# Three chunks instead of four under thirteen first-layer blocks, and two loads moved behind weights: a fused attention + MLP kernel on one core

## The chip, the core and the metric

One core of a Trainium2 chip. The metric is device time in microseconds (us) of one execution; the trace's span, from the first to the last instruction, is 2.0 to 2.2 us shorter in all traces but one. In the traces PE is TensorE, PEld its weight loads, DVE VectorE, ACT ScalarE, POOL GpSimd and SP SyncE.

## The reference

Lightning attention with a decay per head, then a two-layer MLP with an exact Gelu:

```python
# q, k, v: (4 batches, 8 heads, 768, 64); lam: (8,); block = 64
for b in range(nb):
    intra = einsum('bhic,bhjc->bhij', qb, kb) * Dmask      # lam ** (i - j), causal
    out_b = einsum('bhij,bhjd->bhid', intra, vb) + einsum('bhid,bhde->bhie', qb * lam_pow, kv_state)
    kv_state = lam**block * kv_state + einsum('bhsd,bhse->bhde', kb * rev_pow, vb)
x = out.transpose(0, 2, 1, 3).reshape(3072, 512)
h = x @ w_in                                               # 512 -> 2048
out = (0.5 * h * (1 + erf(h / sqrt(2)))) @ w_out           # 2048 -> 512
```

## The kernel before

The kernel works in chunks of 128 positions of one batch: chunk n is batch n % 4, positions from 128 * (n // 4). Four chunks (one of each batch) make a group of 512 tokens, and there are six groups. TensorE runs the MLP of one group as a list of blocks, and between them "visits" do the attention of the next group. Group 0 has nothing to hide its attention under, so its first blocks start on three chunks (384 columns), and the columns of the fourth, chunk 3, are made up later in "leftover" blocks.

```python
    for item in "q0 k1 q1 k2 q2 v1 v2".split():
        load(int(item[1]), item[0])                     # all from POOL, cast to bf16
...
    for piece in [(0, 2), (2, 5), "k", (5, 8), "q", (8, 10), "v", (10, 13), (13, 16)]:
        if piece in ("k", "q", "v"):
            load(3, piece)                              # k3, q3, v3
        else:
            load_w_in(*piece)                           # so many 128-column blocks of w_in
    for s in range(NS):
        load_w_out(s)
...
        split = {0: 10, 1: 8}.get(g, 0)
        blocks = [mm1(kf) for kf in range(NK2)]         # the first `split` on 384 columns
        for i, kf in enumerate(range(0, split, 4)):     # then their last 128 columns, four at a time
            blocks.insert(split + i, mm1(kf, T - C, min(4, split - kf)))
...
    def first_requests():
        for n in (2 * M, 2 * M + 1):                    # M = 4
            request(n)              # SP: kT by DMA transpose; POOL: q_hat; SP: qT by DMA transpose
        for n in range(M, 2 * M):
            decay_k(live[n], nc.gpsimd)                 # k_dec of chunks 4 to 7, on POOL
        prefetch(2 * M + 3)                             # loads of chunks 10 and 11
        for n in (2 * M, 2 * M + 1):
            decay_k(live[n], nc.gpsimd)
    visits = {
        (0, 5): [lambda: kv(0)],                        # before block 5 of group 0: state of chunk 0
        (0, 8): [lambda: transposes(live[3])],
        (0, 9): [lambda: scores(live[3]), lambda: decay_k(live[3], nc.vector)],
        (0, 10): [lambda: kv(1), lambda: outputs(live[3]), lambda: kv(2)],
        (0, 15): [lambda: kv(3)],
...
        (1, 6): [lambda: kv(4, 5)],
        (1, 8): [lambda: kv(6, 7)],
    }
```

`kv(n)` is four matmuls of k_dec and v, then on VectorE a multiplication, with an addition before it from chunk 4 on. k_dec is k times a decay; q_hat is q times a decay, and its DMA transpose is qT. Below "state" is `kv`, and "w_in(5,8)" the piece with blocks 5 to 7.

Of the kernel before, what the change touches and what calls it, by code (L numbers as in the profile page):

```python
# [15 lines left out]
def kernel(  # L16
# [10 lines left out]
    nc = tc.nc  # L27
# [66 lines left out]
        nc.gpsimd.dma_start(w_out_t[:, s * f:(s + 1) * f, :], w_out_r[:, s * f:(s + 1) * f, :])  # L94


    for piece in [(0, 2), (2, 5), "k", (5, 8), "q", (8, 10), "v", (10, 13), (13, 16)]:
        if piece in ("k", "q", "v"):
            load(3, piece)
        else:  # L100
            load_w_in(*piece)
# [53 lines left out]
    live = {}  # L155
# [10 lines left out]
    def decay_k(c, eng):  # L166

        if c.so < NB - 1:
            c.k_dec = work_pool.tile([128, H, D], BF16, tag="kd", name="k_dec", bufs=8)
            eng.tensor_mul(c.k_dec, c.k, lam_m[:, :, None].to_broadcast((128, H, D)))  # L170

    def transposes(c, between=lambda: None):

        t_ps = [bank([128, HP, C], BF16, "m" if c.n < 3 else "sc", "t_ps") for _ in range(2)]
        for dst, src in zip(t_ps, (c.k, c.q)):
            for hp in range(HP):
                nc.tensor.transpose(dst[:, hp, :], src[:, 2 * hp:2 * hp + 2, :], ident)  # L177
            if src is c.k:
                between()
        c.kT = work_pool.tile([128, HP, C], BF16, tag="kT", name="kT")  # L180
        c.qT = work_pool.tile([128, HP, C], BF16, tag="qT", name="qT")
        nc.scalar.copy(c.kT, t_ps[0])
        nc.vector.tensor_mul(c.qT, t_ps[1], lam_q)  # L183
# [9 lines left out]
    def scores(c):  # L193
        sc_ps = [bank([128, HP, C], F32, "sc", f"sc_ps{hi}") for hi in range(2)]
        for hp in range(HP):
            for hi in range(2):
                p = slice(hi * D, (hi + 1) * D)
                nc.tensor.matmul(sc_ps[hi][:, hp, :], c.kT[p, hp, :], c.qT[p, hp, :], start=True, stop=True)  # L198
        c.sc_m = work_pool.tile([128, HP, 2, C], BF16, tag="sc_m", name="sc_m")
        dmask_r = dmask.rearrange("p (hp hi) i -> p hp hi i", hi=2)  # L200
        for hi in range(2):
            nc.vector.tensor_mul(c.sc_m[:, :, hi, :], sc_ps[hi], dmask_r[:, :, hi, :])  # L202
# [18 lines left out]
    def inter(c):  # L221
        c.o_ps = bank([128, HP, C], F32, "sc", "o_ps")
        if c.so > 0:
            for hp in range(HP):
                nc.tensor.matmul(c.o_ps[:, hp, :], states[c.b][:, hp, :], c.qT[:, hp, :],  # L225
                                 start=(hp == 0), stop=False, skip_group_check=True)

    def intra(c):
        for hp in range(HP):
            for hi in range(2):  # L230
                nc.tensor.matmul(c.o_ps[hi * D:(hi + 1) * D, hp, :], c.v[:, 2 * hp + hi, :], c.sc_m[:, hp, hi, :],  # L231
                                 start=(c.so == 0 and hp == 0), stop=True, skip_group_check=True)
        x_o = xT[c.so][:, :, c.b * C:(c.b + 1) * C]
        if c.so < 2:
            nc.scalar.copy(x_o, c.o_ps)  # L235
        else:
            nc.vector.tensor_copy(x_o, c.o_ps)  # L237

    def outputs(c):
        inter(c)  # L240
        intra(c)
# [7 lines left out]
    def mlp_blocks(g):  # L249
        T = M * C  # L250

        split = {0: 10, 1: 8}.get(g, 0)
        x_t = xT[g]
        g_t = g_pool.tile([128, NK2, T], BF16, tag="g", name="g_t")

        def mm1(kf, lo=0, n_kf=1):

            hi = T - C if kf < split and lo == 0 else T
            def run():
                h_ps = bank([128, n_kf, hi - lo], F32, "m", "h_ps")  # L260
                for f in range(n_kf):
                    for ki in range(NK1):
                        w = w_in_t[:, ki, (kf + f) * 128:(kf + f + 1) * 128]
                        nc.tensor.matmul(h_ps[:, f, :], w, x_t[:, ki, lo:hi], start=(ki == 0 and f == 0),  # L264
                                         stop=(ki == NK1 - 1), skip_group_check=True)
                nc.scalar.activation(g_t[:, kf:kf + n_kf, lo:hi], h_ps, ACT.Gelu)  # L266
            return run, 4 * n_kf * (hi - lo)

        om = {}

        def mm2(io, part):
            def run():
                if part == 0:
                    om[io] = bank([128, d_model], F32, "m", "o2_ps")
                for kf in range(part * 4, part * 4 + 4):
                    nc.tensor.matmul(om[io], g_t[:, kf, io * C:(io + 1) * C], w_out_t[:, kf, :],  # L276
                                     start=(kf == 0), stop=(kf == NK2 - 1))
                if part == NK2 // 4 - 1:
                    o_sb = out_pool.tile([128, d_model], F32, tag="o_s", name="o_sb")
                    r = io * S + g * C  # L280
                    nc.scalar.copy(o_sb, om[io])  # L281
                    nc.sync.dma_start(out[r:r + C, :], o_sb)
            return run

        def mm2_cols(io, lo, hi):

            def run():
                o2 = bank([128, hi - lo], F32, "m", "o2_ps")
                for kf in range(NK2):
                    nc.tensor.matmul(o2, g_t[:, kf, io * C:(io + 1) * C], w_out_t[:, kf, lo:hi],  # L290
                                     start=(kf == 0), stop=(kf == NK2 - 1))
                o_sb = out_pool.tile([128, hi - lo], F32, tag=f"o_h{lo}", name="o_sb")
                r = io * S + g * C
                nc.scalar.copy(o_sb, o2)
                nc.sync.dma_start(out[r:r + C, lo:hi], o_sb)
            return run

        parts = NK2 // 4
        blocks = [mm1(kf) for kf in range(NK2)]
        for i, kf in enumerate(range(0, split, 4)):  # L300
            blocks.insert(split + i, mm1(kf, T - C, min(4, split - kf)))
        if g == 0:

            blocks += [(mm2(io, part), 4 * 512) for pair in range(0, M, 2) for part in range(parts)
                       for io in (pair, pair + 1)]
        else:
            last = g == NG - 1
            blocks += [(mm2(io, part), 4 * 512) for io in range(M - last) for part in range(parts)]
            if last:
                blocks += [(mm2_cols(M - 1, lo, hi), NK2 * (hi - lo)) for lo, hi in [(0, 384), (384, d_model)]]  # L310
        return blocks
# [8 lines left out]
    def keep_warm(n, new=True):  # L320

        if new:
            idle_ps[0] = bank([128, 512], F32, "m", "idle_ps")
        for _ in range(n):
            nc.tensor.matmul(idle_ps[0], idle[:, :128], idle, start=True, stop=True)  # L325
# [14 lines left out]
    transposes(live[1], lambda: keep_warm(1, new=False))  # L340
    keep_warm(2)
    outputs(live[0])
    transposes(live[2], lambda: keep_warm(1, new=False))
    nc.scalar.activation(warm, pos, ACT.Gelu)
    scores(live[1])
    keep_warm(1)
    scores(live[2])
    keep_warm(2)
    outputs(live[1])
    keep_warm(2)  # L350
    outputs(live[2])
    keep_warm(4)
    for n in range(M - 1):
# [22 lines left out]
    def kv(*ns):  # L376
        for n in ns:
            next_state(live[n])
            take_state(live[n])

    def first_requests():
        for n in (2 * M, 2 * M + 1):
            request(n)
        for n in range(M, 2 * M):
            decay_k(live[n], nc.gpsimd)
        prefetch(2 * M + 3)
        for n in (2 * M, 2 * M + 1):
            decay_k(live[n], nc.gpsimd)
# [1 line left out]

    visits = {
        (0, 5): [lambda: kv(0)],
        (0, 8): [lambda: transposes(live[3])],
        (0, 9): [lambda: scores(live[3]), lambda: decay_k(live[3], nc.vector)],
        (0, 10): [lambda: kv(1), lambda: outputs(live[3]), lambda: kv(2)],
        (0, 15): [lambda: kv(3)],
        (0, 27): [lambda: transposes(live[4])],
        (0, 29): [lambda: transposes(live[5])],
        (0, 30): [lambda: pair_a(4)],
        (0, 31): [lambda: transposes(live[6])],  # L400
        (0, 32): [lambda: first_requests()],
        (0, 33): [lambda: inter(live[4]), lambda: inter(live[5]), lambda: intra(live[4]), lambda: intra(live[5]),
                  lambda: scores(live[6])],
        (0, 34): [lambda: transposes(live[7]), lambda: outputs(live[6])],
        (1, 1): [lambda: scores(live[7])],
        (1, 4): [lambda: outputs(live[7])],
        (1, 6): [lambda: kv(4, 5)],
# [3 lines left out]
    def pair_a(n):  # L411
        for c in (live[n], live[n + 1]):
            scores(c)
# [68 lines left out]
```

## Time and profile before

| | value |
|---|---|
| time, first three runs | 213.76, 213.80, 214.01 us |
| time and span of the profiled run | 213.84, 211.8 us |
| TensorE busy | 203.2 us (96%) |
| start of the second-layer matmuls of group 0 ("second stage") | 33.69 us |
| from there to the end of the execution | 213.84 - 33.69 = 180.15 us |

The views are in the prediction. In the rows of a timeline L177 is transposes, L198 scores, L210 states, L225 and L231 outputs, L264 the first layer, L276 the second, L325 fillers (`keep_warm` in the kernel: matmuls without use), L170 k_dec and L190 q_hat.

### The profile page before, as it was taken

The numbers are of one execution on the slowest core, as the hardware profiler recorded it, in microseconds if no ns is written. First come the engines' busy times: TensorE is split into PE (matmuls) and PEld (weight loads), VectorE is DVE, ScalarE is ACT, GpSimd is POOL, SyncE is SP. The second block draws the span as 40 slices with busy tenths as digits, with TensorE's granted clock in tenths as the row PEclk, the third lists the DMA queues.
The fourth block names the chain that finished last, engine by engine and source line by source line (L and its number), as shares of the span: only waits on it lengthen the run. The fifth ranks groups of instructions, "written<-read, shape, count | busy, mean of one in ns | idle before, by whom it ended". The sixth has DMA issues, their size and how long they took to land.

```text
span 211.8 us, 3591 instructions
## 1 busy us (share of the span) xinstructions
PE 203.2 (96%) x1469; PEld 106.1 (50%) x1493; DVE 75.7 (36%) x122; ACT 87.7 (41%) x155; POOL 103.7 (49%) x119
## 2 busy tenths in 40 slices
PE   7898899999999999999999999999999999999994
PEld 2444564456674456444465444465444464444442
DVE  4782610173394036840414842244541240000000
ACT  5665553326665211466211465311466311566121
POOL 7994633891997957939795394941000000000000
PEclk9999999999999999999999999999999999999999
DMA  8999999999799799999989999999200012100112
GB/s 89 138 160 182 202 207 189 155 213 156 133 135 113 82 165 137 121 98 187 108 132 134 158 166 155 93 173 159 79 0 3 0 50 99 53 0 0 50 50 99
DMA packets 101327, 24.48 MB, mean 116 GB/s; under 512 B 92992, under 2 KB 98368, under 8 KB 101312
## 3 DMA queue, kind: packets, MB, share of 16 engines
q0 software_dynamic: 79120, 13.51, 86.1%
q1 hardware_dynamic: 22192, 10.76, 26.0%
q8 instruction: 11, 0.18, 0.4%
q14 instruction: 4, 0.03, 0.1%
HBM read 27.27 MB, written 6.29 MB: 158 GB/s over the span
## 4 chain that ended last, share of the span: by engine, by line
PE 87%; POOL 5%; DMA 4%; issue 1%; DVE 1%; ACT 0%; POOLq 0%
PE h_ps L264 37%; PE o_ps L276 37%; DMA w_in_t<-in_moe_w_in_dram 4%; PE sc_ps L198 3%; PE o_ps L231 3%; PE o_ps L225 2%; PE kv_ps L210 2%; POOL k_t L66 2%; PE o_ps L290 2%; POOL q_t L66 1%; PE t_ps L177 1%; POOL v_t L66 1%; POOL w_in_t L90 1%; DVE sc_m L202 1%; DVE qT L183 0%
## 5 line engine op out<-in xcount | busy, mean ns | idle before, releaser
L264 PE MATMUL h_ps<-x_t,w_in_t 128*128 128x512 bf16 (+2 forms) x446 | 86.2, 345 | 1.4 <-DMA w_in_t<-in_moe_w_in_dram 0.6
L276 PE MATMUL o_ps<-w_out_t,g_t 128*128 128x512 bf16 x355 | 81.2, 379 | 1.3 <-issue 1.0
L266 ACT ACTIVATE g_t<-h_ps 128x512 bf16<-128x512 f32 (+2 forms) x101 | 58.2, 577 | 33.8 <-PE h_ps L264 32.6
L264 PEld LDWEIGHTS <-w_in_t 128*128 128x128 bf16 x456 | 40.5, 98 | 41.2 <-DMA w_in_t<-in_moe_w_in_dram 1.1
L276 PEld LDWEIGHTS <-g_t 128*128 128x128 bf16 x368 | 35.0, 98 | 40.8
L202 DVE TENSOR_TENSOR sc_m<-sc_ps,dmask 128x512 bf16<-128x512 f32 x48 | 30.0, 685 | 41.5 <-PE sc_ps L198 41.5
L281 ACT COPY o_sb<-o_ps 128x512 f32<-128x512 f32 x23 | 13.5, 587 | 73.2 <-PE o_ps L276 69.7
L190 POOL TENSOR_TENSOR q_hat<-q_t,lam_p 128x512 bf16<-128x512 bf16 x16 | 16.9, 1056 | 27.3 <-issue 14.3
L66 POOL DMA_DIRECT2D k_t<-in_k_dram x24 | 22.1, 919 | 3.8 <-DMA w_out_t<-in_moe_w_out_dram 1.6
L66 POOL DMA_DIRECT2D q_t<-in_q_dram x24 | 21.6, 900 | 3.5 <-DMA w_out_t<-in_moe_w_out_dram 3.4
L66 POOL DMA_DIRECT2D v_t<-in_v_dram x23 | 20.8, 907 | 3.1 <-DMA w_out_t<-in_moe_w_out_dram 1.6
L170 POOL TENSOR_TENSOR k_dec<-k_t,lam_m 128x512 bf16<-128x512 bf16 x16 | 16.8, 1077 | 0.0
L237 DVE CAST x_t<-o_ps 128x512 bf16<-128x512 f32 x16 | 9.9, 684 | 18.1 <-PE o_ps L231 18.1
L217 DVE TENSOR_TENSOR tmp<-kv_ps,state 128x512 f32<-128x512 f32 x16 | 11.0, 686 | 12.2 <-PE kv_ps L210 12.2
L218 DVE TENSOR_TENSOR state<-tmp,lam_blk 128x512 bf16<-128x512 f32 x16 | 11.5, 719 | 0.6
L325 PE MATMUL idle_ps<-idle 128*128 128x512 bf16 x28 | 9.9, 476 | 1.2 <-DVE idle L106 1.2
L183 DVE TENSOR_TENSOR qT<-t_ps,lam_q 128x512 bf16<-128x512 bf16 x8 | 5.5, 691 | 15.3 <-PE t_ps L177 15.0
L198 PE MATMUL sc_ps<-qT,kT 64*128 64x128 bf16 x192 | 8.0, 217 | 0.7 <-DVE qT L183 0.4
L198 PEld LDWEIGHTS <-kT 64*128 64x128 bf16 x192 | 5.7, 94 | 5.9 <-issue 4.2
L231 PE MATMUL o_ps<-sc_m,v_t 128*64 128x128 bf16 x192 | 8.1, 222 | 0.4 <-DVE sc_m L202 0.2
L231 PEld LDWEIGHTS <-v_t 128*64 128x64 bf16 x192 | 5.9, 109 | 2.9 <-issue 1.7
L235 ACT CAST x_t<-o_ps 128x512 bf16<-128x512 f32 x8 | 4.6, 587 | 5.1 <-PE o_ps L231 5.0
(41 smaller groups left out, 72.1 us busy)
## 6 DMA issues: line engine op xcount, KB each, us to landing
out_dram<-o_sb SPq DMA_DIRECT2D x23, 256.0 KB, 2.2
k_t<-in_k_dram POOLq DMA_DIRECT2D x24, 128.0 KB, 4.7
q_t<-in_q_dram POOLq DMA_DIRECT2D x24, 128.0 KB, 5.7
v_t<-in_v_dram POOLq DMA_DIRECT2D x23, 128.0 KB, 6.5
w_out_t<-in_moe_w_out_dram POOLq DMA_DIRECT2D x4, 512.0 KB, 14.0
w_in_t<-in_moe_w_in_dram POOLq DMA_DIRECT2D x4, 384.0 KB, 9.6
w_in_t<-in_moe_w_in_dram POOLq DMA_DIRECT2D x2, 256.0 KB, 7.8
v_f<-in_v_dram SPq DMA_DIRECT2D x1, 256.0 KB, 3.6
```

The source lines that it names most:

```text
L66: nc.gpsimd.dma_start(raw[n, name], chunk_of(name, n))
L170: eng.tensor_mul(c.k_dec, c.k, lam_m[:, :, None].to_broadcast((128, H, D)))
L190: nc.gpsimd.tensor_mul(q_hat, c.q, lam_p[:, :, None].to_broadcast((128, H, D)))
L198: nc.tensor.matmul(sc_ps[hi][:, hp, :], c.kT[p, hp, :], c.qT[p, hp, :], start=True, stop=True)
L202: nc.vector.tensor_mul(c.sc_m[:, :, hi, :], sc_ps[hi], dmask_r[:, :, hi, :])
L217: nc.vector.tensor_add(tmp, kv_ps, states[c.b])
L218: nc.vector.tensor_mul(new, tmp, lam_blk)
L231: nc.tensor.matmul(c.o_ps[hi * D:(hi + 1) * D, hp, :], c.v[:, 2 * hp + hi, :], c.sc_m[:, hp, hi, :], start=(c.so == 0 and hp == 0), stop=T ...
L264: nc.tensor.matmul(h_ps[:, f, :], w, x_t[:, ki, lo:hi], start=(ki == 0 and f == 0), stop=(ki == NK1 - 1), skip_group_check=True)
L266: nc.scalar.activation(g_t[:, kf:kf + n_kf, lo:hi], h_ps, ACT.Gelu)
L276: nc.tensor.matmul(om[io], g_t[:, kf, io * C:(io + 1) * C], w_out_t[:, kf, :], start=(kf == 0), stop=(kf == NK2 - 1))
L281: nc.scalar.copy(o_sb, om[io])
```

## The change

The intent: take the waits out of group 0's first layer. w_in(5,8) goes ahead of k3, w_in(10,13) ahead of v3; thirteen blocks instead of ten run on three chunks, so that chunk 3's attention has more time; its visits are rearranged for that; and in the start chunk 1's scores are issued ahead of chunk 2's transposes.

```diff
-    for piece in [(0, 2), (2, 5), "k", (5, 8), "q", (8, 10), "v", (10, 13), (13, 16)]:
+    for piece in [(0, 2), (2, 5), (5, 8), "k", "q", (8, 10), (10, 13), "v", (13, 16)]:
@@
-        split = {0: 10, 1: 8}.get(g, 0)
+        split = {0: 13, 1: 8}.get(g, 0)
@@
     outputs(live[0])
+    scores(live[1])
     transposes(live[2], lambda: keep_warm(1, new=False))
     nc.scalar.activation(warm, pos, ACT.Gelu)
-    scores(live[1])
-    keep_warm(1)
-    scores(live[2])
     keep_warm(2)
     outputs(live[1])
-    keep_warm(2)
+    scores(live[2])
+    keep_warm(5)
     outputs(live[2])
@@
-        (0, 8): [lambda: transposes(live[3])],
-        (0, 9): [lambda: scores(live[3]), lambda: decay_k(live[3], nc.vector)],
-        (0, 10): [lambda: kv(1), lambda: outputs(live[3]), lambda: kv(2)],
-        (0, 15): [lambda: kv(3)],
-        (0, 27): [lambda: transposes(live[4])],
...
+        (0, 8): [lambda: transposes(live[3]), lambda: kv(1, 2), lambda: scores(live[3]),
+                 lambda: decay_k(live[3], nc.vector)],
+        (0, 12): [lambda: outputs(live[3])],
+        (0, 17): [lambda: kv(3)],
+        (0, 29): [lambda: transposes(live[4])],
...                     # chunks 4 to 7: each visit one or two blocks later; first_requests stays at 32
```

More of the change, by code (lines that the diff above doesn't have):

```diff
@@ L392 @@
         (0, 5): [lambda: kv(0)],
-        (0, 8): [lambda: transposes(live[3])],
-        (0, 9): [lambda: scores(live[3]), lambda: decay_k(live[3], nc.vector)],
-        (0, 10): [lambda: kv(1), lambda: outputs(live[3]), lambda: kv(2)],
-        (0, 15): [lambda: kv(3)],
-        (0, 27): [lambda: transposes(live[4])],
-        (0, 29): [lambda: transposes(live[5])],
-        (0, 30): [lambda: pair_a(4)],
-        (0, 31): [lambda: transposes(live[6])],
-        (0, 32): [lambda: first_requests()],
-        (0, 33): [lambda: inter(live[4]), lambda: inter(live[5]), lambda: intra(live[4]), lambda: intra(live[5]),
+        (0, 8): [lambda: transposes(live[3]), lambda: kv(1, 2), lambda: scores(live[3]),
[3 more added lines that the diff above has]
+        (0, 29): [lambda: transposes(live[4])],
+        (0, 31): [lambda: transposes(live[5])],
+        (0, 32): [lambda: pair_a(4), lambda: first_requests()],
+        (0, 33): [lambda: transposes(live[6])],
+        (0, 34): [lambda: inter(live[4]), lambda: inter(live[5]), lambda: intra(live[4]), lambda: intra(live[5]),
                   lambda: scores(live[6])],
-        (0, 34): [lambda: transposes(live[7]), lambda: outputs(live[6])],
+        (0, 35): [lambda: transposes(live[7]), lambda: outputs(live[6])],
         (1, 1): [lambda: scores(live[7])],
```

## The prediction

> **What bounds the kernel now.** I read the page first, then the list of waits, then TensorE's timeline from 9 to 64 us, then the landing time of each early transfer.
>
> ```profile
> PE 203.2 (96%) x1469; PEld 106.1 (50%) x1493; DVE 75.7 (36%) x122; ACT 87.7 (41%) x155; POOL 103.7 (49%) x119
> ...
> PE 87%; POOL 5%; DMA 4%; issue 1%; DVE 1%; ACT 0%; POOLq 0%
> ```
>
> TensorE is busy for 203.2 of 211.8 us, and the chain that ended last is 87% TensorE. The rest of that chain is the start: POOL issuing loads up to 11.14 us, then 8.70 us of waiting for w_in, so up to 19.84 us. So only two things can shorten the run: less work on TensorE, or fewer gaps in it. After 33 us the list of waits has one entry for TensorE, "issue" 1.0 us in six pieces. The other gaps are all before 33.5 us, where the change lies. The list of waits for 15 to 33.6 us, PE and its weight loads:
>
> ```profile
> PE h_ps L264 <- DMA w_in_t<-in_moe_w_in_dram: 0.6, 2, 0.4
> PE h_ps L264 <- ACT x_t L235: 0.3, 1, 0.3
> PE o_ps L231 <- DVE sc_m L202: 0.2, 1, 0.2
> ...
> PEld L264 <- DMA w_in_t<-in_moe_w_in_dram: 1.1, 2, 0.6
> ```
>
> These idle times are too short, because the end of each run of matmuls is modelled: the twelve from 17.16 are given 2.12 us, yet the next work starts 1.96 us after them. Distances between starts are safer. TensorE's timeline (start, duration, what, idle before):
>
> ```profile
> 15.51 1.46 PE L264 MATMUL h_ps<-x_t,w_in_t 128*128 128x384 bf16 x8
> 17.16 2.12 PE L264 MATMUL h_ps<-x_t,w_in_t 128*128 128x384 bf16 x12 [0.18 <-DMA w_in_t<-in_moe_w_in_dram]
> 19.12 0.39 PE L210 MATMUL kv_ps<-v_t,k_dec 128*128 128x128 bf16 x4
> 19.89 2.12 PE L264 MATMUL h_ps<-x_t,w_in_t 128*128 128x384 bf16 x12 [0.38 <-DMA w_in_t<-in_moe_w_in_dram]
> 21.85 0.39 PE L177 MATMUL t_ps<-ident,k_t 128*128 128x128 bf16 x4
> ...
> 22.30 0.81 PE L264 MATMUL h_ps<-x_t,w_in_t 128*128 128x384 bf16 x4
> 23.24 0.40 PE L198 MATMUL sc_ps<-qT,kT 64*128 64x128 bf16 x8
> ...
> 25.00 0.38 PE L231 MATMUL o_ps<-sc_m,v_t 128*64 128x128 bf16 x7 [0.21 <-DVE sc_m L202]
> ...
> 26.06 4.12 PE L264 MATMUL h_ps<-x_t,w_in_t 128*128 128x128 bf16 x47 [0.34 <-ACT x_t L235]
> ...
> 33.69 1.67 PE L276 MATMUL o_ps<-w_out_t,g_t 128*128 128x512 bf16 x7
> ```
>
> A block of four 384-wide matmuls takes 0.65 us (twelve take 19.12 - 17.16 = 1.96). A group of 4 or 8 transposes, states, scores or outputs takes 0.22 to 0.45 us. The second matmul stage starts at 33.69 us. Work in this stage: 10 narrow blocks 6.5, four states 0.88, transposes 0.45, scores 0.33, outputs 0.34, 40 leftover matmuls 2.23, 24 wide matmuls 5.18: 15.9 us. The stage lasts 18.18 us, so some 2.2 us of it are gaps (the single ones, from starts: 0.35 for w_in blocks 2 to 4, 0.56 for blocks 5 to 7, 0.29 before chunk 3's scores, 0.49 at its outputs, 0.52 before the leftover columns; sum 2.21).
>
> The gaps at w_in are transfers. Landing is issue start plus time to landing. All these loads leave POOL in one queue and land in its order:
>
> ```profile
> k_t<-in_k_dram POOLq DMA_DIRECT2D x1, 128.0 KB, 7.7
> w_in_t<-in_moe_w_in_dram POOLq DMA_DIRECT2D x1, 384.0 KB, 8.7
> ...
> v_t<-in_v_dram POOLq DMA_DIRECT2D x1, 128.0 KB, 9.4
> w_in_t<-in_moe_w_in_dram POOLq DMA_DIRECT2D x1, 384.0 KB, 10.4
> ```
>
> With issues at 10.27, 11.14, 13.51 and 14.39 us that is k3 at 18.0, w_in(5,8) at 19.84, v3 at 22.9, w_in(10,13) at 24.8. The others, in the same way: w_in(0,2) 15.1, (2,5) 17.1, q3 20.7, (8,10) 22.07, (13,16) 26.7. So a chunk's tensor costs the queue 0.87 us, a 384 KB piece 1.87.
>
> **What the Trainium skill says.** "TensorE: Matmul & The Clock Gate", section "Wait - 56ns, not 53.3ns?": warm matmuls start every N / 2.4 GHz plus about 2.5 ns, 55.6 ns at 128 columns and 215.7 at 512. The trace agrees: 40 leftover matmuls in 2.23 us are 56 ns each, wide ones go at 216. So cutting a block into 384 + 128 is nearly free. "DMA: Bandwidth & Descriptors", section "Two DMAs through the same engine are not ordered": descriptors of one queue start in order, only their completion is not guaranteed in it. The trace shows nine loads landing in issue order, so I move landings by the cost of what is moved. "Perfetto Trace Analysis", section "Tensor Engine Instruction (MATMUL, LD_WEIGHTS)": a matmul's end is estimated by the profiler; hence I count from starts.
>
> **The change, part by part.**
>
> 1. Loads. w_in(5,8) goes ahead of k3 and lands 0.87 earlier, 18.97. k3 then lands at 19.85. q3 and (8,10) have the same bytes ahead of them: 20.7, 22.07. (10,13) goes ahead of v3: 23.95, and v3 24.8. (2,5) and everything after (13,16) stay.
>
> 2. Start. Chunk 1's scores no longer follow chunk 2's qT, so VectorE can mask them from about 10.5 us instead of 11.80. But chunk 2's qT then waits behind those masks (two, 1.29 us, to 11.75), its scores come at 12.45, and its masks end near 14.1 against 14.28. Two more filler matmuls lie under this wait. The first block starts at about 15.35 instead of 15.51. Worth nothing: blocks 2 to 4 still wait for w_in(2,5) at 17.1.
>
> 3. Blocks 2 to 7. From 17.16: state 0 at 19.12, block 5 at 19.33 with its weights there since 18.97. Block 7 ends at 21.29 instead of 21.85: gain 0.56.
>
> 4. Chunk 3's visit at block 8. Transposes at 21.29 (q3 is there), states 1 and 2 (0.45) in place of block 8 (0.65). Before, the scores came 1.39 us after the transposes (21.85 to 23.24), set by the copy and qT (0.69), and so they still do: 22.68. TensorE has only 0.90 us to do meanwhile, so a gap of 0.49 replaces one of 0.29. The scores keep their distance; the gap grows by the 0.20 us by which the two states are shorter than the block they replace.
>
> 5. Blocks 8 to 12. 23.01 to 25.61 for blocks 8 to 11 (block 10 at 24.31, its weights at 23.95: 0.36 to spare). VectorE meanwhile does qT, two states and two masks, to about 25.16. So at 25.61 the masks and v3 (24.8) are both there: the 0.49 gap at the outputs goes. Outputs to 25.95, block 12 to 26.60. ScalarE casts chunk 3's x after block 11's Gelu, 26.20 to 26.79, so the leftovers start at 26.84: a gap of 0.24 in place of 0.52.
>
> 6. Rest. 52 leftover matmuls at 56 ns 2.90, state 3 0.22, 12 wide ones 2.59: the second stage starts at 26.84 + 5.71 = 32.55 instead of 33.69. **Gain 1.14 us.** The extra leftover block and filler are in this count.
>
> 7. Second stage. Chunks 4 to 7 move by one or two blocks, because the list is one block longer. Fourth chunk's transposes: 32.55 + 9 x 0.865 = 40.3, against 40.60 after eight blocks; k4, q4 land at 37.9 and 38.9. Fifth 42.5 (q5 41.6), sixth 45.2 (q6 44.2), seventh 48.8 (q7 47.8). All still land ahead by about 1 us. w_out's third and fourth quarters, at 34.4 and 36.9, are wanted at 36.0 and 37.7. One block less lies between the sixth chunk's transposes and outputs 4 and 5; the four masks before them took 2.48 us from 0.43 after the scores' start, so end 2.91 after, and inter(5) comes 3.08 after: it just fits. So the gain passes to the end: after that the only gaps are issue.
>
> Sum: 213.8 - 1.14 = 212.7 us, ratio 0.995.
>
> **The rivals.**
> First, new waits take the gain. w_in(10,13) has 0.36 us to spare, v3 0.8, masks 4 and 5 about 0.2, q5 to q7 about 1. For: all these margins rest on landings good to perhaps 0.1 us. Against: each can cost only its own overrun. Two of them slipping by 0.3 would leave 213.3.
> Second, the w_in wait is hidden anyway: if (5,8) isn't faster behind (2,5), because k3's descriptors overlap with it, gap 0.56 stays and only outputs and leftovers gain, some 0.5 us: 213.3. Against it speaks the even spacing of landings.
> Third, the gap before chunk 3's scores proves smaller, as states 1 and 2 and the copies might overlap better; then w_in(10,13) at 23.95 holds block 10, which caps the extra at 0.36: 212.3.
> Fourth, the reordered start costs: chunk 2's scores now wait for its qT, and if they come later than I think, so does the first block. It can be up to 0.35 us late at no cost, as that is the wait for w_in(2,5) behind it; 0.5 us more would leave 213.2. Against it: I expect the start earlier, by 0.16.
>
> **Range and chances.** The three new waits pull upwards, the cap at 0.36 limits the lower side: 212.3 to 213.4. 2% would be 4.3 us, twice all the gaps of this stage (2.21), so faster by over 2% is all but excluded. Slower by 2% needs a stall of 5 us that no landing suggests.
>
> **What would show it.** Right: no wait for w_in before block 5, transposes of chunk 3 near 21.3, scores near 22.7 with a gap before them, leftovers near 26.8, first w_out matmul near 32.5, and stages after that equally long. Wrong: a wait for w_in at block 10 or for v3 at chunk 3's outputs, w_in(5,8) landing after 19.3, or new TensorE gaps between 40 and 52 us.

## The result, and the profile after

The changed kernel took 213.37 us (median of 212.88, 213.17, 213.56 and 213.68); the kernel before, with one run more, 213.79. The ratio is 0.9976, 95% interval 0.9954 to 0.9998. Ratios here are the mean time of one kernel's fast runs over that of the other's of the same rounds, so not quite the ratio of the medians quoted. Executions over 1.5% slower than the fastest of the same kernel are left out of the means. I had forecast 1.1 us of gain, ratio 0.995; the medians show 0.42. Where a verdict asks for 2%, every run of this study is "same"; what follows is about differences of half a percent and less.

TensorE's timeline of the changed kernel, to set against that of before:

```profile
15.26 3.58 PE L264 MATMUL h_ps<-x_t,w_in_t 128*128 128x384 bf16 x20
18.68 0.39 PE L210 MATMUL kv_ps<-v_t,k_dec 128*128 128x128 bf16 x4
19.54 2.12 PE L264 MATMUL h_ps<-x_t,w_in_t 128*128 128x384 bf16 x12 [0.47 <-DMA w_in_t<-in_moe_w_in_dram]
21.50 0.39 PE L177 MATMUL t_ps<-ident,k_t 128*128 128x128 bf16 x4
...
22.89 0.40 PE L198 MATMUL sc_ps<-qT,kT 64*128 64x128 bf16 x8 [0.34 <-DVE qT L183]
...
25.92 0.41 PE L231 MATMUL o_ps<-sc_m,v_t 128*64 128x128 bf16 x8
26.27 3.84 PE L264 MATMUL h_ps<-x_t,w_in_t 128*128 128x384 bf16 x56
...
32.76 7.93 PE L276 MATMUL o_ps<-w_out_t,g_t 128*128 128x512 bf16 x36
...
58.02 0.83 PE L210 MATMUL kv_ps<-v_t,k_dec 128*128 128x128 bf16 x8
```

Up to the second stage this is the predicted picture, 0.21 us late from block 5 on: w_in(5,8) landed at 19.49 instead of the predicted 18.97, and block 5 waited for it. (Landings here and below are read from the packed traces.) So one of the prediction's signs of being wrong is in this trace (the landing after 19.3), and one of those of being right is not (no wait for w_in before block 5). From there every distance is as worked out (transposes at 21.50, scores 22.89, outputs 25.92, second stage 32.76; the prediction has 21.29, 22.68, 25.61, 32.55, so only the outputs are 0.10 later still, and that is made up again). The second stage starts 0.93 us earlier than before.

Then it loses some of that. The last row shows it: states 6 and 7, at 58.02 us, take 0.83 instead of the 0.61 that the same row has in the kernel before:

```profile
58.95 0.61 PE L210 MATMUL kv_ps<-v_t,k_dec 128*128 128x128 bf16 x8
```

The chain that ended last no longer runs along TensorE there. Its pieces from 45 to 60 us (start, length, what):

```profile
46.20 7.08 DMA q_t<-in_q_dram
...
53.35 1.04 POOL q_hat L190
54.40 1.63 POOL k_dec L170 x2
...
56.35 2.06 POOL k_dec L170 x2
...
58.45 0.40 PE kv_ps L210 x4
```

Read upwards: state 7 (58.45) waits for the fourth k_dec on POOL; the four k_dec (chunks 4 to 7) wait for q_hat 9, which stands ahead of them in POOL's program; q_hat 9 waits for the load of q of chunk 9, which lands 7.08 us after its issue at 46.20, at 53.28. TensorE is not in this chain, so its coming earlier doesn't bring it forward. Here is POOL before the change and after, from 47 us, in this order:

```profile
50.84 1.04 POOL L190 TENSOR_TENSOR q_hat<-q_t,lam_p 128x512 bf16<-128x512 bf16 x1 [3.29 <-DMA q_t<-in_q_dram]
52.98 1.04 POOL L190 TENSOR_TENSOR q_hat<-q_t,lam_p 128x512 bf16<-128x512 bf16 x1 [1.10 <-DMA q_t<-in_q_dram]
53.98 4.04 POOL L170 TENSOR_TENSOR k_dec<-k_t,lam_m 128x512 bf16<-128x512 bf16 x4
```

```profile
51.16 1.04 POOL L190 TENSOR_TENSOR q_hat<-q_t,lam_p 128x512 bf16<-128x512 bf16 x1 [2.63 <-ACT x_t L235]
53.35 1.04 POOL L190 TENSOR_TENSOR q_hat<-q_t,lam_p 128x512 bf16<-128x512 bf16 x1 [1.15 <-DMA q_t<-in_q_dram]
54.35 4.04 POOL L170 TENSOR_TENSOR k_dec<-k_t,lam_m 128x512 bf16<-128x512 bf16 x4
```

Before, the four ended at 53.98 + 4.04 = 58.02 us and state 7's matmuls came at 59.17 (58.95 for states 6 and 7, plus 0.22). That is a slack of 1.15 us that no list of waits shows, because nothing waited. The predicted gain was 1.14. Of this slack the change used 0.93 by bringing TensorE forward; POOL's four k_dec moreover ended 0.37 later, as q9 landed 0.37 later in this trace.

### The profile page after: what moved, and what is told of

Same layout as the page of the kernel before. It is cut to its first block, busy times and chain, and to the rows that moved or that the text cites. A ratio compares the mean times of both kernels' runs of the same rounds, so it can differ in the third digit from the quotient of the medians.

```text
span 211.1 us, 3620 instructions
## 1 busy us (share of the span) xinstructions
PE 203.2 (96%) x1483; PEld 106.9 (51%) x1507; DVE 76.4 (36%) x122; ACT 87.7 (42%) x156; POOL 104.0 (49%) x119
## 4 chain that ended last, share of the span: by engine, by line
PE 70%; DMA 15%; POOL 11%; issue 2%; ACT 0%; POOLq 0%
PE o_ps L276 31%; PE h_ps L264 30%; DMA w_out_t<-in_moe_w_out_dram 7%; DMA w_in_t<-in_moe_w_in_dram 4%; DMA q_t<-in_q_dram 3%; POOL k_t L66 3%; POOL q_t L66 2%; PE sc_ps L198 2%; POOL v_t L66 2%; PE o_ps L231 2%; POOL k_dec L170 2%; PE o_ps L225 2%; PE o_ps L290 2%; PE kv_ps L210 1%; POOL w_out_t L94 1%
## 5 line engine op out<-in xcount | busy, mean ns | idle before, releaser
L264 PEld LDWEIGHTS <-w_in_t 128*128 128x128 bf16 x468 | 41.2, 98 | 40.5 <-DMA w_in_t<-in_moe_w_in_dram 1.0
L190 POOL TENSOR_TENSOR q_hat<-q_t,lam_p 128x512 bf16<-128x512 bf16 x16 | 17.6, 1100 | 26.9 <-issue 13.4
L218 DVE TENSOR_TENSOR state<-tmp,lam_blk 128x512 bf16<-128x512 f32 x16 | 12.4, 772 | 0.5
L182 ACT COPY kT<-t_ps 128x512 bf16<-128x512 bf16 x8 | 4.7, 583 | 5.4 <-PE t_ps L177 5.3
```

What stands on the lines that cost most here:

```text
L190: nc.gpsimd.tensor_mul(q_hat, c.q, lam_p[:, :, None].to_broadcast((128, H, D)))
L218: nc.vector.tensor_mul(new, tmp, lam_blk)
L264: nc.tensor.matmul(h_ps[:, f, :], w, x_t[:, ki, lo:hi], start=(ki == 0 and f == 0), stop=(ki == NK1 - 1), skip_group_check=True)
```

## The experiments

Each call is one batch of runs on one chip, with the kernel before beside them. **Theory K:** the gain is made before the second stage, as predicted, and cut at state 7, which waits for POOL's k_dec. **Rival U:** the shortfall and the spread of the runs come from loads before 33 us. A third question was whether the new order of loads costs the queue time, as w_in(5,8) came 0.52 us after its predicted landing.

### First call: the chain on POOL, and the loads

**after_again**: the changed kernel, unchanged.

> The changed kernel once more. The record has 212.88 to 213.68 us for it, against 213.76 to 214.01 before. Theory K: state 7 waits for k_dec of chunk 7 on POOL, which waits (through q_hat 9) for the landing of q of chunk 9; in the first trace q9 landed at 53.30 and the state started at 58.45, 0.2 late. If K holds, the start of state 7 is again within 0.1 us of the end of POOL's fourth k_dec, and q9's landing plus about 5.2 us gives it; ratio to before 0.996 to 0.999. Rival U: the spread comes from w_in(5,8) and v3 before 33 us; then the second stage's start (32.76) moves by as much as the time does and state 7 has no wait. Third point: w_in(5,8) landed 2.76 us after (2,5) where I had reckoned 1.87; if this belongs to the order it is again 2.5 or more, if it was chance it is about 1.9.

Measured: 213.12 us median, ratio 0.9962 (0.9945 to 0.9980), but the profiled run 215.0. Its trace: second stage at 33.11 us, (5,8) at 19.58, 1.91 us behind (2,5), where the first trace had 2.82. The order does not fix this distance: over the thirteen traces with the new order it is 1.90 to 2.95, on the mean 2.28, so the 1.87 that I reckoned with is its lower end. q9 landed at 54.58, and TensorE shows at the states:

```profile
56.75 0.40 PE L210 MATMUL kv_ps<-v_t,k_dec 128*128 128x128 bf16 x4
57.75 0.40 PE L210 MATMUL kv_ps<-v_t,k_dec 128*128 128x128 bf16 x4 [0.60 <-POOL k_dec L170]
59.29 0.39 PE L210 MATMUL kv_ps<-v_t,k_dec 128*128 128x128 bf16 x4
60.20 0.40 PE L210 MATMUL kv_ps<-v_t,k_dec 128*128 128x128 bf16 x4 [0.53 <-POOL k_dec L170]
```

Four states that used to come in two close pairs are torn apart by two waits, at state 5 and at state 7. From the second stage to the end it took 215.0 - 33.11 = 181.89 us instead of 180.15: 1.7 us lost here. K holds in this run, and state 5 waits too, which I hadn't named. The fourth k_dec ended 5.57 us after q9's landing, not 5.2: it took 1.49 us instead of 1.04, with a multiplication of state 4 on VectorE beside it (more on this in the last section).

**a_kdec_first**: the changed kernel with POOL's k_dec moved up.

```diff
     def first_requests():
-        for n in (2 * M, 2 * M + 1):
-            request(n)
         for n in range(M, 2 * M):
             decay_k(live[n], nc.gpsimd)
+        for n in (2 * M, 2 * M + 1):
+            request(n)
         prefetch(2 * M + 3)
```

> Changed kernel, with k_dec of chunks 4 to 7 issued on POOL ahead of the two q_hat. POOL idled 2.63 and 1.15 us before the q_hats, so the four (4.04 us) run from about 48.6 to 52.7 and state 7 can't wait for them. Theory K: the 0.94 us gained by the second stage's end passes to the end; faster than the changed kernel by 0.2 to 0.6 us, ratio to before 0.994 to 0.996, spread of the runs down to some 0.3 us. Rival U: as the changed kernel, within 0.1 us, same spread.

Measured: 213.98 us (median of the five fast runs, 212.68 to 214.98; a sixth, 216.74, is slow), ratio 0.9996 (0.9962 to 1.0030). Neither theory's number. The wait at the states is gone (57.86 us, 0.61 long), but there is another:

```profile
PE sc_ps L198 <- DMA qT<-q_hat: 1.0, 1, 1.0
```

The scores of chunks 8 and 9 waited for qT 9. The transposes of kT 9 and qT 9, from issue to landing in this kernel:

```profile
kT<-k_t SPq DMA_TRANSPOSE x1, 6.7
qT<-q_hat SPq DMA_TRANSPOSE x1, 7.3
```

In the changed kernel both took 2.4. With k_dec out of the way, POOL issued the loads of chunks 10 and 11 at 54.18 instead of 58.33 us, beside the transposes. So the move mended one wait and made another; next call.

**b_kdec_first**: the same edit in the kernel before.

> The same move in the kernel before. There POOL's fourth k_dec ended at 58.02 and state 7 began at 59.17 us: 1.15 us to spare. Theory K: no change, ratio 0.999 to 1.001. If the move gains here too, it works through something else than state 7 (earlier loads of chunks 10 and 11, say), and K isn't what it shows in the changed kernel.

Measured: 214.95 us, ratio 1.0049 (1.0020 to 1.0077); I had said no change. The trace shows no wait after 33 us and a span of 212.0, close to before's 211.8; the profiled run's 215.0 has 3.0 us outside the span, where every other profiled run has 2.0 to 2.2. Two more of the six runs have 3.1 and 3.3, and so have two runs of the kernel before in later calls (216.21 us with a span of 213.1, 215.71 with 212.0), so it doesn't belong to this edit alone. What it is stays open. The spans, with a median of 212.45 against 211.9, are 0.55 longer too. The move gains nothing here, where there was slack, as expected; the loss was not expected, and only in part explained (qT 9 took 5.9 us in this trace, but TensorE didn't wait for it).

**a_old_loads**: the changed kernel with the old order of loads (the diff's first hunk undone).

> Changed kernel with the old order of loads (k3 ahead of w_in(5,8), v3 ahead of w_in(10,13)). If, as I predicted, a 384 KB piece costs the queue 1.87 us wherever it stands, (5,8) lands about 19.8, (10,13) about 24.8 and holds block 10, and the second stage starts at about 33.1 instead of 32.76. If the new order itself slows the queue (q9 0.35 us later in the changed kernel), then here q9 lands near 52.95, (5,8) near 19.8, state 7 doesn't wait, and the time is as the changed kernel's, ratio 0.997.

Measured: 213.26 us, ratio 0.9972 (0.9957 to 0.9987), all runs within 0.35. (5,8) at 19.83, second stage at 33.10, no wait at the states, rest 213.34 - 33.10 = 180.24 us. With less gain before the second stage, all of it arrives: within 0.14 us of the changed kernel in the same call (213.12), whose second stage starts earlier on the mean of its three traces (32.70), though not in this call's (33.11). That is as K has it.

### Second call: mending POOL without the collision, and parts alone

**a_kdec_mid**: k_dec put into POOL's idle time, loads as late as before.

```diff
     def first_requests():
-        for n in (2 * M, 2 * M + 1):
-            request(n)
-        for n in range(M, 2 * M):
-            decay_k(live[n], nc.gpsimd)
-        prefetch(2 * M + 3)
+        for n in (M, M + 1):
+            decay_k(live[n], nc.gpsimd)
+        request(2 * M)
+        decay_k(live[M + 2], nc.gpsimd)
+        request(2 * M + 1)
+        decay_k(live[M + 3], nc.gpsimd)
         for n in (2 * M, 2 * M + 1):
             decay_k(live[n], nc.gpsimd)
+        prefetch(2 * M + 3)
```

> Changed kernel. POOL's k_dec of chunks 4 and 5 go into its idle time ahead of q_hat 8, that of 6 between the two q_hat, 7, 8 and 9 behind q_hat 9, and only then the loads of chunks 10 and 11, so that these start at about 57 us, as in the changed kernel (58.3), and not at 54.2 as in a_kdec_first. Theory K2: state 7 waits for POOL in the changed kernel, and a_kdec_first lost its gain only because its early loads made the transposes of kT 9 and qT 9 take 6.7 and 7.3 us instead of 2.4. Then here: no wait at state 7, transposes at 2.4 to 3 us, 212.6 to 213.0 us, ratio to before 0.994 to 0.996, all runs within 0.6 us. Rival: another transfer decides (v3 or w_in(5,8)); then as the changed kernel, 213.1 with a spread of 0.8 us or more.

Measured: 212.80 us, 212.69 to 212.93, ratio 0.9962 (0.9949 to 0.9975; the kernel before had 213.71 in this call). POOL now, from 48 us:

```profile
48.30 2.06 POOL L170 TENSOR_TENSOR k_dec<-k_t,lam_m 128x512 bf16<-128x512 bf16 x2
50.96 1.04 POOL L190 TENSOR_TENSOR q_hat<-q_t,lam_p 128x512 bf16<-128x512 bf16 x1 [0.60 <-DMA q_t<-in_q_dram]
51.95 1.04 POOL L170 TENSOR_TENSOR k_dec<-k_t,lam_m 128x512 bf16<-128x512 bf16 x1
53.13 1.04 POOL L190 TENSOR_TENSOR q_hat<-q_t,lam_p 128x512 bf16<-128x512 bf16 x1
54.13 3.04 POOL L170 TENSOR_TENSOR k_dec<-k_t,lam_m 128x512 bf16<-128x512 bf16 x3
```

The q_hat are where they were, the fourth k_dec ends at 55.17 instead of 58.4, and no wait at the states is left. Second stage at 32.69, rest 180.24. As K2 had it; qT 9 took 4.3 us to land, more than the 2.4 to 3 I gave, but in time.

**a_kdec_late**: a_kdec_first with `prefetch` behind the k_dec of chunks 8 and 9.

> a_kdec_first with k_dec of chunks 8 and 9 ahead of the loads, so that the loads start near 56.3 instead of 54.2 while the q_hat stay as late as there (52.2 and 53.2). If the loads were what slowed the transposes: kT 9 and qT 9 land sooner, qT 9 by 60.5 us, no wait at the scores of chunks 8 and 9, time near a_kdec_mid's, about 212.8 to 213.2. If the late q_hat were the cause: the wait at these scores stays at about 1 us and the time at 214.

Measured: 212.64 us, ratio 0.9957 (0.9942 to 0.9971). The q_hat were as late as in a_kdec_first (52.1), the loads at 56.1; kT 9 and qT 9 took 4.0 and 5.0 us, and the scores had no wait of TensorE's matmuls. (The time is a little below what I gave, and qT 9 landed at 60.78, just after.) So it was the early loads that cost a_kdec_first its gain.

**b_new_loads**: only the diff's first hunk, in the kernel before.

> The kernel before with only the new order of loads. (5,8) at 19.1 to 19.6 instead of 19.84, but v3 at 24.9 to 25.4 instead of 22.9, and the outputs of chunk 3 want it at about 24.2: they wait, the leftovers start near 26.2, the second stage at 33.7 to 34.0. So no gain alone: ratio 1.000 to 1.002. Second point: (13,16) lands at about 27.1 as in the three runs with the new order, if the order costs the queue some 0.35 us; at 26.6 to 26.8 if it doesn't.

Measured: 214.10 us, ratio 1.0020 (0.9994 to 1.0046): no gain alone, as said. The profiled run was the luckiest of the six (213.04): (5,8) at 18.38, the second stage at 32.94, outside what I gave; the wait that I expected is there, 0.48 us for v3 at chunk 3's outputs. (13,16) landed at 26.08, not at 27.1. Over all traces it landed at 26.85 us with the new order (13 traces, mean) and 26.96 with the old (5). So these traces show no cost of the order to the queue.

**b_split**: only thirteen blocks and their visits, in the kernel before.

> The kernel before with only the thirteen blocks and their visits (old loads, old start). If the visits make the gain and the start is worth nothing: as a_old_loads, 213.1 to 213.4 us, ratio 0.997, second stage at 33.1, no wait at state 7, narrow spread. If the start is worth 0.15 to 0.25 us, the ratio is 0.998 and the second stage begins at 33.3.

Measured: 213.44 us (213.0 to 214.13), ratio 0.9995 (0.9974 to 1.0017): just above what I gave, the ratio well above it, and the second stage at 33.41, 0.3 late. In this trace (2,5) and (5,8) landed at 17.40 and 20.14, so blocks 5 to 7 started at 20.19 and the rest follows at the distances of the changed kernel. No wait at the states. Inconclusive as to the start.

### Third call: the states' slack by itself, and each part on top

**a_state**: the changed kernel with one visit moved.

```diff
-        (1, 8): [lambda: kv(6, 7)],
+        (1, 9): [lambda: kv(6, 7)],
```

> Changed kernel with states 6 and 7 one leftover block (0.9 us) later in TensorE's list, nothing else: POOL, the loads and their order stay. Theory K: in the changed kernel state 7 was wanted at 58.24 us and POOL's k_dec of chunk 7 ends 5.1 us after q 9 lands (52.8 to 53.3 in eight of nine traces), so it has no slack; 0.9 us more gives it that. Then no wait at state 7, 212.6 to 213.0 us, ratio to before 0.995 to 0.9965, as a_kdec_mid. If a_kdec_mid gained by its earlier k_dec of 8 and 9 or its other load times instead, this stays at the changed kernel's 213.1 to 213.2.

Measured: 212.89 us, ratio 0.9964 (0.9941 to 0.9988). In its trace, no wait of TensorE's matmuls after the second stage, which began at 32.12; rest 180.28. It spreads over 1.06 us though. State 5 still has no slack, which would fit.

**a_state_fill**: a_state with block 8 ahead of chunk 3's scores.

```diff
-        (0, 8): [lambda: transposes(live[3]), lambda: kv(1, 2), lambda: scores(live[3]),
-                 lambda: decay_k(live[3], nc.vector)],
+        (0, 8): [lambda: transposes(live[3]), lambda: kv(1, 2)],
+        (0, 9): [lambda: scores(live[3]), lambda: decay_k(live[3], nc.vector)],
```

> a_state with block 8 moved ahead of chunk 3's scores, into the gap of 0.34 to 0.49 us before them (the prediction's step 4). If the gap is on the path: 0.15 to 0.35 us faster than a_state (w_in(10,13), landing at 24.2 on the mean, may take back up to 0.2), the second stage at about 32.4. If the next wait takes it (weights at block 10, or the masks at the outputs): equal within 0.1.

Measured: 212.89 us, ratio 0.9963, equal. From block 5 to the second stage it took 32.73 - 19.57 = 13.16 us, against 32.12 - 18.90 = 13.22 in a_state: only 0.06 gained. The gap before the scores is gone, but block 8 now waited for w_in(8,10), which landed at 22.52 when TensorE was ready for it at 22.42, and block 10 for w_in(10,13), at 24.44 when it was due at 24.31. The next wait took the gain, as the second half of the expectation has it.

**a_state_old_start**: a_state with the old start.

> a_state with the start of the kernel before. Prediction's step 2: worth nothing, because blocks 2 to 4 wait for w_in(2,5) at about 17.1 whichever start there is: within 0.1 us of a_state. If the landing of (2,5) is early (16.4 to 16.8 in three of ten traces), the first block's 0.15 to 0.25 us show: ratio 0.0005 to 0.001 above a_state's.

Measured: 212.95 us, 0.06 above a_state by medians; but the ratio is 0.9974, 0.0010 above a_state's, which is the other answer. The runs don't decide it. The traces show no earlier first block: it starts at 15.60 us on the mean of the thirteen with the new start, and at 15.46 in the five with the old.

**a_state_old_loads**: a_state with the old loads.

> a_state with the old order of loads. w_in(5,8) landed at 19.16 us on the mean of six traces with the new order and 19.97 in four with the old; so blocks 5 to 7 start at about 19.9 to 20.1 instead of 19.4, and the time is 0.4 to 0.6 us above a_state's, ratio about 0.998 (a_old_loads was 0.9972, where state 7 had its slack because TensorE came later). If the loads aren't what carries the gain, it is within 0.2 of a_state.

Measured: 213.38 us, ratio 0.9988, 0.49 above a_state, as expected, with runs that overlap (a_state reaches 213.46). With the states' slack given, the new order of loads is worth about half a microsecond; without it (the changed kernel against a_old_loads, in the first call) 0.14.

### Fourth call: the size, side by side

**after_third**: the changed kernel.

> The changed kernel, third time, beside its cures on one chip. If the waits of states 5 and 7 for POOL are what is missing: median 0.3 to 0.6 us above a_kdec_mid_again's, and the time of the profiled run is its second stage's start + 180.2 us + the waits of PE and its weight loads at the states. If not, within 0.15 us of it.

Measured: 213.50 us, ratio 0.9991 (0.9956 to 1.0025). The clearest trace of all. Loads were quick (second stage at 32.24 us, 1.45 before the kernel before's), q9 landed at 53.13 as usual, and

```profile
55.76 0.39 PE L210 MATMUL kv_ps<-v_t,k_dec 128*128 128x128 bf16 x4
56.30 0.40 PE L210 MATMUL kv_ps<-v_t,k_dec 128*128 128x128 bf16 x4 [0.15 <-POOL k_dec L170]
57.83 0.39 PE L210 MATMUL kv_ps<-v_t,k_dec 128*128 128x128 bf16 x4
58.74 0.40 PE L210 MATMUL kv_ps<-v_t,k_dec 128*128 128x128 bf16 x4 [0.53 <-POOL k_dec L170]
```

State 7 at 58.74: not earlier than in the first trace (58.45), although TensorE was 0.5 us ahead of it. Rest 213.42 - 32.24 = 181.18 us, so 1.0 lost, as the weight loads' wait for k_dec says (1.0 in this trace). The four k_dec took 4.49 us here, and not 4.04: 0.45 of state 7's delay is theirs, not q9's.

**a_kdec_mid_again**: as a_kdec_mid.

> Again 0.9 to 1.1 us below the kernel before (ratio 0.995 to 0.996), all runs within 0.5 us; the profiled run's time is its second stage's start + 180.2 +- 0.1 us.

Measured: 213.22 us, ratio 0.9965 (0.9931 to 0.9999). Half a microsecond below the kernel before by medians, less than expected, and 0.28 below after_third, just under the 0.3 to 0.6 given there. The spread, 0.70, is above what I gave as well. The profiled run had slow loads (second stage 32.91) and 180.58 us after it: no wait at the states, but 0.3 for q of chunk 6, which landed at 46.37, later than in any other trace.

**a_both_states**: states 4 and 5 moved too.

```diff
-        (1, 6): [lambda: kv(4, 5)],
-        (1, 8): [lambda: kv(6, 7)],
+        (1, 7): [lambda: kv(4, 5)],
+        (1, 9): [lambda: kv(6, 7)],
```

> Changed kernel with states 4 and 5 one block later (0.65 us) and 6 and 7 one leftover block later (0.9 us). a_state moved 6 and 7 only; there state 5 still began when POOL's second k_dec ended, and the runs spread over 1.06 us. If the slack of the states is all there is: as a_kdec_mid_again within 0.15 us, spread below 0.7 us. If it still spreads over 1 us or more, something else varies in the runs.

Measured: 213.28 us (213.03 to 213.67), ratio 0.9973: 0.06 from a_kdec_mid_again, spread 0.64. The slack of the states alone does what the new order on POOL does, as far as these runs resolve it. In the trace no wait at the states, 32.88 + 180.25.

**a_late_fill**: a_kdec_late with a_state_fill's hunk.

> a_kdec_late (the fastest so far) with block 8 ahead of chunk 3's scores. a_state_fill showed 0.06 us between block 5 and the second stage (13.16 against 13.22), so at most 0.1 us better than a_kdec_late was: 212.5 to 212.7 us, ratio 0.995.

Measured: 212.67 us, ratio 0.9942 (0.9907 to 0.9977): the best of all against its own call, 1.04 us below the kernel before. How it stands against a_kdec_late (0.9957) isn't resolved. Its runs spread over 1.63 us. Its trace is the other half of a_state_fill: w_in was early ((8,10) at 21.60, (10,13) at 23.52), so block 8 in the gap is worth 0.36 here (31.81 - 18.95 = 12.86 us against 13.22), and the second stage starts earliest of all. Then the next slack ends, that of q of chunk 6, which landed at 45.55:

```profile
45.59 0.40 PE L177 MATMUL t_ps<-ident,q_t 128*128 128x128 bf16 x4 [0.39 <-DMA q_t<-in_q_dram]
```

The rest to the end is 180.83 us, 0.6 more than without a wait.

## Why the prediction was wrong, by its own steps

| | second stage starts | rest to the end | waits at the states (weight loads) |
|---|---|---|---|
| before | 33.69 | 180.15 | none |
| changed, first trace | 32.76 | 180.41 | 0.2 |
| changed, after_again | 33.11 | 181.89 | 1.8 |
| changed, after_third | 32.24 | 181.18 | 1.0 |
| a_kdec_mid | 32.69 | 180.24 | none |
| a_both_states | 32.88 | 180.25 | none |

**Steps 1 to 6 held on the mean.** Over the nine traces with the changed first layer and new loads, and without block 8 moved or the old start, the second stage starts at 32.62 us on the mean; step 6 said 32.55. w_in(5,8) landed at 19.12 with the new order (13 traces, 18.30 to 19.64) and 20.03 with the old (5): 0.91 apart, step 1 said 0.87. From block 5 to the second stage it took 13.21 to 13.23 us in all nine; steps 3 to 6 have 32.55 - 19.33 = 13.22. So the gap before chunk 3's scores, the outputs without a wait and the leftovers came at the predicted distances. The landing of w_in(5,8) is the weak point: in these nine it was at 19.23 on the mean, 0.26 later than step 1 said, in four after 19.3, and in three block 5 waited for it. That block 5 still starts at 19.40, 0.07 late, owes something to luck: step 3 had 0.36 us of room, and (2,5) landed at 16.98 instead of 17.1. Step 2's earlier first block isn't in the traces; that the start doesn't decide the time is not contradicted, but not settled (a_state_old_start).

**Step 7 failed,** in the sentence "So the gain passes to the end: after that the only gaps are issue." I had checked in it the transposes, the masks and w_out, but not the states of chunks 4 to 7. Their other input is made by POOL, off TensorE's chain, at a time that is set by the landing of q9. In the kernel before it was ready 1.15 us ahead of state 7 and 1.41 ahead of state 5 (56.02 against 57.43), and the change was to bring TensorE forward by 1.14. Where q9 was a little late, or the loads before 33 us a little early, part of the gain was cut: 0.3, 1.7 and 1.0 us in the three traces of the changed kernel. The sign of it, gaps between 40 and 52 us, looked too early: they are at 56 to 60. A second part came on top in two of them: state 4's multiplication on VectorE now lies beside POOL's k_dec (in the kernel before it began at 58.36, after the last of them), and the last k_dec took 1.49 us instead of 1.04. That the one lengthened the other is read from their lying side by side; no run tests it.

**Rival 1 was the right family, with the wrong members.** "New waits take the gain" named w_in(10,13), v3, the masks and q5 to q7, and none of these held TensorE in the three traces of the changed kernel. They did in others: w_in(10,13) in a_state_fill, and q of chunk 6 in a_kdec_mid_again and a_late_fill. Rival 2: behind (2,5) the piece did land earlier, by 0.91 on the mean. Rival 3: the gap before the scores didn't get smaller. Rival 4: the first block did start later than I expected, at 15.60 on the mean. That cost nothing where blocks 2 to 4 waited for w_in(2,5); in the two traces where this landed at 16.1 to 16.2 (a_state and a_late_fill), block 2 came 0.6 us after it.

**How much it is on the mean.** The 17 runs of the changed kernel have a median of 213.35 us, the 49 runs of the kernel before 213.76: gain 0.41. a_kdec_mid's twelve runs: 212.91, gain 0.85. By this the wait would be some 0.44 of the 0.73 us that are missing from the forecast 1.14; but it is an estimate, as the runs are of different chips, and the changed kernel gained 0.79 in the first call and 0.21 in the fourth. Side by side, in the fourth call alone, the cure is worth 0.28, with overlapping runs. Of the other 0.3 us, 0.07 are the second stage's start (32.62 for 32.55) and 0.08 the profiled run of the kernel before, which lies that much above its median; the rest I can't place.

That the wait is a cause is shown three ways: in the traces, by POOL's order (a_kdec_mid), and by moving the states alone (a_both_states). With either cure no trace waits for k_dec, and the rest to the end is back at 180.2 us, but for the 0.3 at q of chunk 6. How much the wait costs in an average run isn't settled, as only three runs of the changed kernel have a trace.

## What to carry to other kernels

When a change brings an engine forward, look up for everything that it consumes later by how much the producer was early, and what sets that producer's time. Such a slack is in no list of waits, and a gain stops at the smallest one; when that is widened, it stops at the next (w_in at blocks 8 and 10, then q of chunk 6). An instruction whose inputs are long there should not stand in an in-order engine's program behind one that waits for a late transfer: POOL idled 2.63 and 1.15 us ahead of k_dec whose k had landed. And see what else the engine will then do earlier: the loads that followed k_dec ran into transposes and took the gain back once.

## What the Trainium skill lacked or had wrong

- "DMA: Bandwidth & Descriptors", section "Rules for kernel authors": it says that a transpose next to ordinary DMAs needs nothing. That is about right results; it gives no cost, and no page that I read has a figure for it. Here kT 9 and qT 9 took 2.4 us from issue to landing in the changed kernel, and 6.7 and 7.3 in a_kdec_first, whose loads were issued 4.15 us earlier, beside them.
- The same page, section "Two DMAs through the same engine are not ordered": its order of starts is said of one queue of one DMA engine, which the prediction left out; nothing, it says, orders DMAs across the 16 engines. Here POOL's loads nevertheless landed in issue order in all 18 traces. What it lacks is their spread: the same load behind the same bytes, w_in(5,8) with the new order, landed between 18.30 and 19.64 us, and q9 between 52.73 and 54.58 over all kernels here. Margins of a few tenths on a landing were not margins here.
- "SBUF - State Buffer", section "Who interferes with whom": it says that a VectorE instruction with two SBUF inputs contends with a GpSimd instruction that reads SBUF. Nothing wrong in it: in the changed kernel the state's multiplication (two SBUF inputs) beside POOL's k_dec took 1.52 us instead of 0.69, and in after_third the four k_dec 4.49 instead of 4.04, while the addition that reads PSUM stayed at 0.68. I hadn't thought of it: states and k_dec that come to lie side by side lengthen the very chain that the states wait for.
- No page that I read has the time outside the span, or why it is 3.0 us in the trace of b_kdec_first and up to 3.7 in a run of the kernel before (2.0 to 2.2 in all other traces).
